# Causal attention and a cosine layer on one core: v loaded a step sooner, the last pair's transposes moved up

## Chip, core and metric

The kernel runs on one core of a Trainium2 chip. The metric is the device time of one execution in microseconds (us). TensorE (PE) multiplies and transposes; a transpose is a matmul with an identity matrix. VectorE (DVE), ScalarE (ACT) and GpSimd (POOL) work beside it, and SyncE (SP) only issues transfers between HBM and the on-chip memory. Each engine runs its own instructions in the order in which they are written; semaphores hold an engine back where it needs what another makes.

## What is computed

Two parts stand one behind the other: causal attention over 4 batches of 12 heads (448 tokens, 64 columns each), and a layer of two matrix products with g = h cos(h) between them.

```python
def _attn_ref(q, k, v):                         # (4, 12, 448, 64), float32
    scores = scale * np.matmul(q, k.transpose(0, 1, 3, 2))
    scores = np.where(mask, -1000000000.0, scores)
    scores = scores - np.max(scores, axis=-1, keepdims=True)
    attn = np.exp(scores)
    attn = attn / (np.sum(attn, axis=-1, keepdims=True) + 1e-09)
    return np.matmul(attn, v).astype(np.float32)

def _moe_ref(x, w_in, w_out):                   # x: (1792, 768), w_in: (768, 2048)
    h = x @ w_in
    g = h * np.cos(h)
    return (g @ w_out).astype(np.float32)
```

## The kernel before

The program is written out by hand: the order in the source is the order on each engine. `attention` is a generator; each `yield` ends a step, and the loop that drives it puts a piece of weight conversion for the second part behind each step.

The 4 x 12 heads make N = 24 pairs of heads. Step i works on three pairs at once:

- `scores(i)` (matmuls at L360), `masked` (DVE, L369: mask, running minimum) and `exps` (ACT, L376) make the probabilities of pair i in one of three tiles `pb`.
- `av(i - 2)` (L410) multiplies the transposed probabilities of pair i - 2 with its v, `divide` (DVE, L437 to L439) divides by the sums, `turn_out` (L448) transposes the outputs, and `finish` (ACT, L464 and L465) and `finish_hi` (POOL, L470 and L471) store them as x of the second part. The products, the ones column that gives the sums and the turned outputs all lie in PSUM banks 0 and 1.
- `transpose_in(i + 2)` (L316) transposes q and k of pair i + 2, which `evac_in` copies to SBUF in the next step.
- `tp(i - 1)` (L393) transposes the probabilities of pair i - 1 in two groups into PSUM, and `evac_tp` (L320 on DVE, L322 on ACT) copies them to a tile `pm`.

On TensorE a step is scores, av, transpose_in, tp, turn_out. Steps 0 to 2 are put together differently, since the pipeline fills. Behind the last scores, in steps 23 to 25, `fill` puts matmuls of the second part (the first 36, L570 to L572) between what is left of attention; step 26 runs the rest of these.

SP issues the loads. In step i stand `load_qk(i + 3)` (L257: two issues for k, two for q, 64 runs of partitions with pieces of 256 bytes, into one of three buffers in the tile `land`), `load_v(i - 1)` (L266: two issues into `vn`, one of three buffers; for even pairs also L273: two issues into `vo`, one of two buffers, for pairs i and i + 1), and behind them, from the driving loop, now and then a piece of a weight (L117, L122), a store of converted weights (L204, L206) or of raw ones (L1347). At the end of step 22 the driving loop adds two weight loads of 768 KB (L117) into `land`, and behind steps 23 to 25 ACT makes masks from them (L166, L168, L170).

Before step 0 `keep_warm` issues matmuls on a tile of zeros (L287).

Of the kernel before, what the change touches and what calls it, by code (L numbers as in the profile page):

```python
# [21 lines left out]
def kernel(  # L22
# [205 lines left out]
    def attention(filler_of, postponed):  # L228
        with (
# [19 lines left out]
            def half(h):  # L249
                return slice(h * R, (h + 1) * R)  # L250
# [34 lines left out]
            def keep_warm(n):  # L285
                for _ in range(n):
                    nc.tensor.matmul(  # L287
                        banks8[:, 0, 0:P], lhsT=warm, rhs=warm, start=True, stop=True
                    )

            keep_warm(44)
            ident = cst.tile([P, P], F32, name="ident")
            make_identity(nc, ident)

# [16 lines left out]
            def transpose_in(i, bs, order=None):  # L311
                for h in range(2):
                    qkt[i, h] = flat[:, 2 * h + i % 2, 0:S], banks8[:, bs[h], 0:S]
                for c, h in order or [(c, h) for c in range(NM) for h in range(2)]:
                    o = qkt[i, h][1].rearrange("p (r c) -> p c r", c=NM)
                    nc.tensor.transpose(o[:, c], nat[i][half(h), c], ident[half(h), half(h)])  # L316
# [7 lines left out]
            def evac_in(i, h, dve=False):  # L324
                evac(*qkt[i, h], dve)
# [14 lines left out]
            def open_step(i):  # L340
                prob[i] = prob_t[i % 3]
                stats[i] = at.tile([P, 8], F32, tag="stat", bufs=3, name="stat")
# [31 lines left out]
            def exps(i, *ms):  # L374
                for m in ms:
                    nc.scalar.activation(  # L376
                        probs(i, m), probs(i, m), AF.Exp, scale=-1.0, bias=stats[i][:, col(m)]
                    )
# [19 lines left out]
            def evac_tp(i, g, bs, h, dve=False):  # L398
# [2 lines left out]
                    banks8[:, bs[h], 0 : NM * R], dve,  # L401
                )

            def av(i):
                (vn, vo), pt = vals.pop(i), ptr[i]

                def add(m, j, y, lhsT, rhs, start=False, stop=False):
                    b, n, h = PLACE[m]
                    c = (2 * n + j) * E1
                    nc.tensor.matmul(  # L410
                        banks8[half(h), b, c : c + E1], lhsT=lhsT, rhs=rhs, start=start, stop=stop
                    )

                for j in range(2):
                    for y in range(2):
                        for a, ms in enumerate(LAST):
                            m, ys = ms[y], half(y)
                            g, n = spots[ms[0], NM]
                            add(
                                m, j, y, pt[ys, g, j ^ SWAP[m], n],  # L420
                                vo[ys, a, i % 2, j] if y else vn[ys, m // 2, j], start=j == 0,
                            )
                pieces = [(7, 6, k) for k in range(3)] + [(5, 4, k) for k in range(2)] + [(2, 3, 0)]
                for x, (ma, mb, k) in enumerate(pieces):
                    for j in range(2):
                        for m in (ma, mb):
                            g, n = spots[m, k]
                            add(
                                m, j, 0, pt[:, g, j ^ SWAP[m], n], vn[:, k, j],
                                stop=j == 1 and x in (2, 5),  # L430
                            )

            def divide(i):
                o = banks8[:, 0:2, 0 : 4 * E1].rearrange("p b (n e) -> p b n e", e=E1)
                r = at.tile([P, 2, 4, 1], F32, tag="r", bufs=2, name="r")
                t = outs[i] = at.tile([P, 2, 4, D], F32, tag="on", bufs=2, name="on")
                nc.vector.tensor_scalar(r, o[:, :, :, D:E1], 1e-9, None, op0=ALU.add)  # L437
                nc.vector.reciprocal(r, r)
                nc.vector.tensor_tensor(t, o[:, :, :, 0:D], r.to_broadcast([P, 2, 4, D]), op=ALU.mult)  # L439

            def turn_out(i):
                t = outs[i].rearrange("p b n d -> p b (n d)")
                for x in range(4):
                    for h, ms in enumerate((ROW[1::2], ROW[::2])):
                        if x < len(ms):
                            b, n, _ = PLACE[ms[x]]
                            c = (T0, 4 * R)[h] + x * R
                            nc.tensor.transpose(  # L448
                                banks8[:, 1 - h, c : c + R],
                                t[half(h), b, n * P : (n + 1) * P], ident[half(h), half(h)],  # L450
                            )

# [8 lines left out]
            def finish(i):  # L461
                xf = at.tile([P, S], F32, tag="xf", bufs=2, name="xf")
                x = xf.rearrange("p (n r) -> p n r", r=R)
                nc.scalar.copy(x[:, 1::2], banks8[:, 1, T0 : T0 + 3 * R].rearrange("p (n r) -> p n r", r=R))  # L464
                nc.scalar.copy(x[:, 0::2], banks8[:, 0, 4 * R : 8 * R].rearrange("p (n r) -> p n r", r=R))  # L465
                return xf

            def finish_hi(i, xf):
# [11 lines left out]
                    pass  # L480

            TB_ = (2, 3)
            transpose_in(0, TB_)
            evac_in(0, 1)
            evac_in(0, 0, True)
            keep_warm(10)
            load_v(0)
            for i in range(N + 4):
                cur, prev, old = i < N, 0 < i <= N, 0 <= i - 2 < N
                G1, G2 = (7, 4), (5, 6)  # L490
                if i == 1:
                    G1, G2 = (0, 1), TB_
                elif i >= N - 1:
                    G1, G2 = TB_, (4, 5)
                while postponed:
                    postponed.pop(0)()
                if i + 3 < N:
                    load_qk(i + 3)
                if 1 < i <= N:
                    load_v(i - 1)  # L500
                if cur:
                    open_step(i)
                    scores(i)
                if i == 0:
                    masked(i, 4, 3)
                    exps(i, 4, 3)
                    masked(i, 7, 6)
                    exps(i, 7)
                    transpose_in(1, TB_)
                    evac_in(1, 0, True)  # L510
                    evac_in(1, 1)
                    keep_warm(8)
                    exps(i, 6)
                    masked(i, 5, 1, 2)
                    exps(i, 5, 1, 2)
                    yield i
                    continue
                if i == 1:
                    transpose_in(2, TB_)
                    masked(i, 4, 3, 7, 6, 5, 1, 2)  # L520
                    exps(i, 4, 3)
                    evac_in(2, 0)
                    evac_in(2, 1)
                    exps(i, 7)
                elif cur:
                    if 2 < i < N - 1:
                        evac_in(i + 1, 0)
                        evac_in(i + 1, 1)
                    masked(i, 4, 3, 7, 6, 5, 1, 2)
                    exps(i, 4, 3, 7, 6, 5, 1, 2)  # L530
                    if i == 2:
                        transpose_in(3, TB_)
                        evac_in(3, 0, True)
                        evac_in(3, 1, True)
                if i == N + 2:
                    run(extra[0])
                if old:
                    av(i - 2)
                    divide(i - 2)
                if 1 < i < N - 2:  # L540
                    transpose_in(i + 2, TB_)
                if i == N:
                    fill(8)
                if prev:
                    open_ptr(i - 1)
                    tp(i - 1, 0, G1)
                    evac_tp(i - 1, 0, G1, 0, True)
                    evac_tp(i - 1, 0, G1, 1)
                    if i == 1:
                        exps(i, 6, 5)  # L550
                    tp(i - 1, 1, G2)
                    evac_tp(i - 1, 1, G2, 1)
                    evac_tp(i - 1, 1, G2, 0, i % 2 == 0 or i < 4)
                if i == 1:
                    exps(i, 1, 2)
                if N - 2 < i < N + 2:
                    fill((4, 4, 6)[i + 1 - N])
                if old:
                    turn_out(i - 2)
                    xf = finish(i - 2)  # L560
                    finish_hi(i - 2, xf)
                yield i

    def m1_sum(ring, g, fi, t0, n, hv):
        x, t = x_part(t0, n)
# [844 lines left out]
```

## Time and profile before

| | us |
|---|---|
| median of the three timed runs | 610.51 |
| the three runs | 607.86, 610.51, 611.37 |
| the profiled execution | 608.23 |
| its span, first to last instruction | 606.1 |

The profiled execution is some 2 us longer than its span: the span runs from the first to the last instruction. All times of rows are counted from the start of the span. Attention takes the first 165 us or so; the rest is the second part. The granted TensorE clock has a mean of 0.997 of full speed over the span.

### The profile page before, as it was taken

How to read it: one execution, taken by the hardware profiler on the slowest of the kernel's cores; microseconds unless marked ns; L12 is line 12 of the kernel's file. 1: busy time of each engine (PE TensorE's matmuls, PEld its weight loads, DVE VectorE, ACT ScalarE, POOL GpSimd, SP SyncE). 2: the span in 40 equal slices, each digit the busy share in tenths (PEclk: the TensorE clock that was granted, in tenths of full speed). 3: DMA queues.
4: the chain of work that ended last, by engine and by line, in shares of the span. 5: the costliest groups of instructions: out<-in, count | busy, mean ns of one | idle time of the engine just before them, and what ended most of it. 6: DMA issues, size and time to landing. Idle time of an engine off the chain costs nothing.

```text
span 606.1 us, 15320 instructions
## 1 busy us (share of the span) xinstructions
PE 587.0 (97%) x5912; PEld 544.5 (90%) x5912; DVE 454.7 (75%) x955; ACT 401.3 (66%) x785; POOL 398.3 (66%) x426
## 2 busy tenths in 40 slices
PE   8999898898999999999999999999999999999996
PEld 7888787787799989899999999999999999999996
DVE  5988698886477787877777777853387887887786
ACT  5999798987566797877778777732534644654540
POOL 0235344535258787877878777844579779878994
PEclk9999999999999999999999999999999999999999
DMA  8768667676037879796968878589988548648105
GB/s 158 161 156 183 162 154 201 156 181 175 10 131 247 300 211 339 241 351 194 345 239 284 297 228 322 193 303 391 391 331 292 195 149 303 209 158 305 58 1 156
DMA packets 127096, 134.30 MB, mean 222 GB/s; under 512 B 75152, under 2 KB 111360, under 8 KB 127024
## 3 DMA queue, kind: packets, MB, share of 16 engines
q1 hardware_dynamic: 118400, 106.69, 57.3%
q0 software_dynamic: 4928, 24.78, 11.1%
q10 hardware_dynamic: 3696, 1.87, 1.2%
q8 instruction: 46, 0.75, 0.5%
q14 instruction: 26, 0.21, 0.1%
HBM read 83.36 MB, written 49.94 MB: 220 GB/s over the span
## 4 chain that ended last, share of the span: by engine, by line
PE 73%; DVE 11%; DMA 8%; ACT 3%; SPq 3%; issue 2%; POOL 1%; DVEq 0%; ACTq 0%
PE banks L666 18%; PE banks L1115 12%; PE banks L1095 12%; PE banks L571 6%; PE banks L572 6%; PE banks L570 6%; PE banks L410 4%; PE banks L360 3%; DMA vo<-in_v_dram 2%; DVE pb L369 2%; PE banks L1132 2%; PE banks L1019 2%; DMA vn<-in_v_dram 2%; SPq L257 2%; DVE pm L320 2%
## 5 line engine op out<-in xcount | busy, mean ns | idle before, releaser
L654 DVE TENSOR_TENSOR acc<-acc,banks 128x768 f32<-128x768 f32 (+1 forms) x122 | 112.6, 932 | 43.1 <-PE banks L666 32.9
L666 PE MATMUL banks<-w,gh 128*128 128x384 f32 x512 | 110.0, 335 | 0.1
L666 PEld LDWEIGHTS banks<-w,gh 128*128 128x128 f32 x512 | 90.7, 188 | 2.2 <-DVE acc L654 0.8
L571 PE MATMUL banks<-xa,w 128*128 128x512 f32 x192 | 75.5, 393 | 0.0
L572 PE MATMUL banks<-xa,w 128*128 128x512 f32 x192 | 75.0, 391 | 0.0
L570 PE MATMUL banks<-xa,w 128*128 128x512 f32 x192 | 74.9, 390 | 0.0
L376 ACT ACTIVATE pb<-pb,stat 128x256 f32<-128x256 f32 (+6 forms) x168 | 71.4, 522 | 3.0 <-DVE stat L369 2.9
L666 PE MATMUL banks<-w,gl 128*128 128x384 f32 x256 | 65.1, 335 | 0.0
L369 DVE CUSTOM_DVE_ANT_0 pb<-banks,mask 128x256 f32<-128x256 f32 (+6 forms) x168 | 59.8, 420 | 5.0 <-PE banks L360 5.0
L690 POOL TENSOR_TENSOR w<-ct,w 128x768 fp32r<-128x768 f32 x28 | 51.9, 1853 | 16.0 <-ACT w L689 15.9
L470 POOL CAST xa<-xf 128x448 fp32r<-128x448 f32 (+1 forms) x18 | 9.6, 532 | 75.6 <-ACT xf L465 75.6
L578 ACT ACTIVATE ni<-banks 128x512 int32<-128x512 f32 (+1 forms) x64 | 34.4, 537 | 33.4 <-PE banks L572 20.2
L410 PE MATMUL banks<-vn,pm 128*64 128x65 f32 (+1 forms) x1344 | 51.3, 227 | 3.9 <-DMA vn<-in_v_dram 2.4
L597 POOL TENSOR_TENSOR gl<-r,gh 128x512 fp32r<-128x512 f32 x32 | 41.5, 1299 | 16.7 <-ACT gh L596 16.5
L580 DVE SCALAR_TENSOR_TENSOR r<-ni,banks 128x512 f32<-128x512 int32 (+1 forms) x56 | 35.0, 626 | 22.6 <-ACT ni L578 21.9
L410 PEld LDWEIGHTS banks<-vn,pm 128*64 128x64 f32 (+1 forms) x1344 | 46.2, 140 | 6.4 <-ACT pb L376 1.9
L582 ACT ACTIVATE r<-r 128x512 f32<-128x512 f32 (+1 forms) x56 | 32.8, 585 | 22.6 <-DVE r L580 22.0
L666 PEld LDWEIGHTS banks<-w,gl 128*128 128x128 f32 x256 | 46.4, 188 | 0.0
L585 DVE SCALAR_TENSOR_TENSOR r<-r,banks 128x512 f32<-128x512 f32 (+1 forms) x56 | 35.1, 626 | 13.6 <-ACT r L583 13.6
L1095 PE MATMUL banks<-xb,bb 128*128 128x384 f32 x234 | 44.8, 334 | 0.0
L360 PE MATMUL banks<-flat 64*64 64x64 f32 (+5 forms) x768 | 42.1, 356 | 2.1 <-ACT flat L322 0.6
L360 PEld LDWEIGHTS banks<-flat 64*64 64x64 f32 x768 | 32.7, 133 | 11.4 <-DVE pm L320 3.7
(142 smaller groups left out, 1445.2 us busy)
## 6 DMA issues: line engine op xcount, KB each, us to landing
bb<-w_in_d SPq DMA_DIRECT2D x48, 384.0 KB, 5.2
land<-in_moe_w_in_dram SPq DMA_DIRECT2D x14, 768.0 KB, 6.3
land<-in_moe_w_out_dram SPq DMA_DIRECT2D x14, 768.0 KB, 5.7
w_out_d<-w POOLq DMA_DIRECT2D x14, 768.0 KB, 5.8
big<-w_out_d SPq DMA_DIRECT2D x25, 384.0 KB, 5.2
w_in_d<-w POOLq DMA_DIRECT2D x7, 768.0 KB, 4.2
raw_d<-ct POOLq DMA_DIRECT2D x14, 384.0 KB, 7.5
land<-in_k_dram SPq DMA_DIRECT2D x45, 112.0 KB, 3.6
```

The lines of the kernel that those rows point to most:

```text
L360: nc.tensor.matmul(place(m)[heads(j ^ SWAP[m]), c : c + z - a], lhsT=qt[heads(j), (m - 1) * R : m * R], rhs=kt[heads(j), a:z], start=banks ...
L369: nc.vector.tensor_tensor_reduce(out=probs(i, m), in0=place(m), in1=mask[:, z : z + m * R], scale=-scale, scalar=3.0e38, op0=ALU.add, op1= ...
L376: nc.scalar.activation(probs(i, m), probs(i, m), AF.Exp, scale=-1.0, bias=stats[i][:, col(m)])
L410: nc.tensor.matmul(banks8[half(h), b, c : c + E1], lhsT=lhsT, rhs=rhs, start=start, stop=stop)
L570: yield nc.tensor.matmul(hv, lhsT=wh[:, f], rhs=x[:, 0, cc, t], start=(cc == 0), stop=False)
L571: yield nc.tensor.matmul(hv, lhsT=wh[:, f], rhs=x[:, 1, cc, t], start=False, stop=False)
L572: yield nc.tensor.matmul(hv, lhsT=wl[:, f], rhs=x[:, 0, cc, t], start=False, stop=(cc == NCC - 1))
L654: nc.vector.tensor_tensor(d, d, o, op=ALU.subtract)
L666: nc.tensor.matmul(o[:, e, 0:EH], lhsT=a[:, cs], rhs=w[:, e * EH : (e + 1) * EH], start=(x == 0), stop=(x == 5),)
L690: nc.gpsimd.tensor_tensor(w[:, 1], tf, f32(w[:, 0]), op=ALU.subtract)
L1095: nc.tensor.matmul(o, lhsT=w[:, u, k * P : (k + 1) * P], rhs=x[k][:, v], start=k + m == 0, stop=k == K - 1 and m == 2,)
L1115: nc.tensor.matmul(o[:, b % 2, 0:EH], lhsT=g_ops[i][u][:, c * P : (c + 1) * P], rhs=wouts[g, i][:, v], start=(x == 0), stop=(x == 2),)
```

## The change

There are three parts.

- `load_v(i)` is called in step i, where `load_v(i - 1)` was. The vn buffer of pair i was last read by av(i - 3), in step i - 1, so that the issue now has a wait on TensorE.
- Step 23 transposes the probabilities of pair 23 itself, behind the outputs of pair 21 and two fillers, group 1 into banks 4 and 5, group 0 into 2 and 3. The product of pair 23 and its turned output lie in banks 4 and 5 instead of 0 and 1 (`obank`). Then av(22), av(23), the outputs of pair 22, four fillers, the outputs of pair 23; the fillers that are left follow.
- In steps 0 to 2 some work changes places: k is transposed ahead of q, with zero matmuls behind each (32, 9, 8 and 6 where there were 44, 10 and 8), and the transposes of pair 0's probabilities stand in steps 1 and 2, a group in each.

```diff
-            keep_warm(44)
+            keep_warm(32)
...
+            def obank(i):
+                return 4 if i == N - 1 else 0
+
             def av(i):
-                (vn, vo), pt = vals.pop(i), ptr[i]
+                (vn, vo), pt, ob = vals.pop(i), ptr[i], obank(i)
...
+            def evac_out(i, g, bs, *dve):
+                for h in range(2):
+                    evac_tp(i, g, bs, h, h in dve)
+
+            def put_out(i):
+                turn_out(i)
+                finish_hi(i, finish(i))
...
                 if i + 3 < N:
                     load_qk(i + 3)
-                if 1 < i <= N:
-                    load_v(i - 1)
-                if cur:
-                    open_step(i)
-                    scores(i)
+                if i:
+                    load_v(i)
+                open_step(i)
+                scores(i)
...
+                if i == N - 1:
+                    fill(4)
+                put_out(i - 2)
+                if i == N - 1:
+                    fill(2)
+                    open_ptr(i)
+                    tp(i, 1, (4, 5))
+                    evac_out(i, 1, (4, 5), 0)
+                    tp(i, 0, TB_)
+                    evac_out(i, 0, TB_, 0)
                 yield i
+            take_postponed()
+            av(N - 2)
+            divide(N - 2)
+            yield N
+            take_postponed()
+            av(N - 1)
+            divide(N - 1)
+            put_out(N - 2)
+            fill(4)
+            put_out(N - 1)
+            yield N + 1
+            take_postponed()
+            run(extra[0])
```

On SP's queue, before, steps 18 to 20 read as follows: k and q of pair 21, vn of pair 17, a raw store and a weight piece, k and q of pair 22, vn and vo of pair 18, k and q of pair 23, vn of pair 19 (a number behind vn or vo names the buffer, x2 the two heads).

```order
L257 DMA land<-in_k_dram 64x7x64 x2
L257 DMA land<-in_q_dram 64x7x64 x2
L266 DMA vn_90<-in_v_dram 128x3x64 x2
L1347 DMA raw_d<-ct 128x256
L122 DMA st<-in_moe_w_out_dram 128x512
L257 DMA land<-in_k_dram 64x7x64 x2
L257 DMA land<-in_q_dram 64x7x64 x2
L266 DMA vn_88<-in_v_dram 128x3x64 x2
L273 DMA vo_92<-in_v_dram 64x4x64 x2
L257 DMA land<-in_k_dram 64x7x64 x2
L257 DMA land<-in_q_dram 64x7x64 x2
L266 DMA vn_89<-in_v_dram 128x3x64 x2
```

The same steps on SP's queue in the changed kernel, from k and q of pair 21 to vn and vo of pair 20.

```order
L257 DMA land<-in_k_dram 64x7x64 x2
L257 DMA land<-in_q_dram 64x7x64 x2
L266 DMA vn_88<-in_v_dram 128x3x64 x2
L273 DMA vo_92<-in_v_dram 64x4x64 x2
L1379 DMA raw_d<-ct 128x256
L122 DMA st<-in_moe_w_out_dram 128x512
L257 DMA land<-in_k_dram 64x7x64 x2
L257 DMA land<-in_q_dram 64x7x64 x2
L266 DMA vn_89<-in_v_dram 128x3x64 x2
L257 DMA land<-in_k_dram 64x7x64 x2
L257 DMA land<-in_q_dram 64x7x64 x2
L266 DMA vn_90<-in_v_dram 128x3x64 x2
```

The vn and vo of pair 18 (vn_88, vo_92) stood behind q of pair 22 and now stand ahead of its k.

On TensorE, before, in step 24: the last fillers ahead of the transposes of pair 23's probabilities (pb_160), these, four fillers, the turned outputs of pair 22 and the start of the product of pair 23 (vn_90).

```order
L572 MATMUL banks<-xa,w_500 128x512
L570 MATMUL banks<-xa,w_500 128x512
L571 MATMUL banks<-xa,w_500 128x512
L572 MATMUL banks<-xa,w_500 128x512
L393 MATMUL banks<-ident,pb_160 128x64 x28
L570 MATMUL banks<-xa,w_500 128x512
L571 MATMUL banks<-xa,w_500 128x512
L572 MATMUL banks<-xa,w_500 128x512
L570 MATMUL banks<-xa,w_500 128x512
L448 MATMUL banks<-ident,on 128x64 x7
L410 MATMUL banks<-vn_90,pm 64x65 x2
L410 MATMUL banks<-vo_92,pm 64x65 x2
```

In the changed kernel, from the last of four fillers and the turned outputs of pair 21 in step 23 to the start of the product of pair 23 (L602 to L604 are the fillers, L452 the turned outputs, L413 the product; the tile pb_148 is that of pair 23).

```order
L602 MATMUL banks<-xa,w_497 128x512
L452 MATMUL banks<-ident,on 128x64 x7
L603 MATMUL banks<-xa,w_497 128x512
L604 MATMUL banks<-xa,w_497 128x512
L393 MATMUL banks<-ident,pb_148 128x64 x28
L413 MATMUL banks<-vn_89,pm 64x65 x2
L413 MATMUL banks<-vo_92,pm 64x65 x2
L413 MATMUL banks<-vn_89,pm 64x65 x2
L413 MATMUL banks<-vo_92,pm 64x65 x2
L413 MATMUL banks<-vn_89,pm 64x65 x24
L413 MATMUL banks<-vn_90,pm 64x65 x2
L413 MATMUL banks<-vo_92,pm 64x65 x2
```

The transposes of pair 23 moved ahead of the product of pair 22, and the two last products stand one behind the other.

## Rows read from the trace of the kernel before

**Rows 1.** Page, section 1: engine, busy us, share of span, instructions.

```profile
PE 587.0 (97%) x5912; PEld 544.5 (90%) x5912; DVE 454.7 (75%) x955; ACT 401.3 (66%) x785; POOL 398.3 (66%) x426
```

**Rows 2.** Busy by stretch, TensorE: stretch, length, busy (count), granted clock, DMA share, GB/s.

```profile
160.00:300.00 140.00, 139.87 (x708) 1.00 0.74 247
```

**Rows 3.** TensorE in order of time: start, us, line, out<-in, count [idle before <-releaser].

```profile
21.96 1.75 PE L360 MATMUL banks<-flat 64*64 64x256 f32 x32
...
92.47 1.75 PE L360 MATMUL banks<-flat 64*64 64x256 f32 x32
...
95.94 0.65 PE L316 MATMUL banks<-ident,land 64*128 64x64 f32 x14
...
97.84 1.75 PE L360 MATMUL banks<-flat 64*64 64x256 f32 x32
...
101.46 0.27 PE L410 MATMUL banks<-vo,pm 64*64 64x65 f32 x1 [1.47 <-DMA vo<-in_v_dram]
...
127.59 0.65 PE L316 MATMUL banks<-ident,land 64*128 64x64 f32 x14
...
129.49 1.75 PE L360 MATMUL banks<-flat 64*64 64x256 f32 x32
```

**Rows 4.** SP's issues in order of time, steps 15 and 19.

```profile
92.11 1.29 SPq L257 DMA_DIRECT2D land<-in_k_dram  x2
93.45 1.28 SPq L257 DMA_DIRECT2D land<-in_q_dram  x2
94.78 2.02 SPq L266 DMA_DIRECT2D vn<-in_v_dram  x2
96.84 1.27 SPq L273 DMA_DIRECT2D vo<-in_v_dram  x2
...
118.15 1.29 SPq L257 DMA_DIRECT2D land<-in_q_dram  x2
```

**Rows 5.** One line, L257, 21 to 126 us: count, ns min/median/max, first and last.

```profile
L257 SPq EVENT_SEMAPHORE  x18: 17/17/17, 21.4 to 122.4; - x18
```

**Rows 6.** Transfers issued from 118.1 to 119.4: count, KB, median us to landing.

```profile
land<-in_q_dram SPq DMA_DIRECT2D x2, 112.0 KB, 4.3
```

**Rows 7.** TensorE in order of time, the tail.

```profile
143.80 1.09 PE L393 MATMUL banks<-ident,pb 64*128 64x64 f32 x28
...
147.16 0.33 PE L410 MATMUL banks<-vn,pm 64*64 64x65 f32 x4 [0.75 <-ACT xf L465]
148.13 0.59 PE L410 MATMUL banks<-vo,pm 64*64 64x65 f32 x3 [0.64 <-DMA vo<-in_v_dram]
...
157.36 0.27 PE L410 MATMUL banks<-vn,pm 64*64 64x65 f32 x2 [0.75 <-ACT xf L465]
...
159.30 0.50 PE L571 MATMUL banks<-xa,w 128*128 128x512 f32 x1
...
160.89 0.46 PE L448 MATMUL banks<-ident,on 64*128 64x64 f32 x7
161.28 0.50 PE L571 MATMUL banks<-xa,w 128*128 128x512 f32 x1
...
164.59 0.39 PE L570 MATMUL banks<-xa,w 128*128 128x512 f32 x1
```

**Rows 8.** Busy by stretch, TensorE, the tail (columns as in rows 2).

```profile
145.00:148.80 3.80, 2.38 (x27) 1.00 0.74 115
148.80:152.30 3.50, 3.50 (x56) 0.51 0.02 5
```

**Rows 9.** ACT in order of time, step 23.

```profile
144.76 1.37 ACT L322 COPY pm<-banks 128x448 f32<-128x448 f32 x3
...
146.72 0.38 ACT L465 COPY xf<-banks 128x256 f32<-128x256 f32 x1
```

**Rows 10.** SP's weight loads, and landing of transfers issued from 138.5 to 143.4.

```profile
137.56 0.97 SPq L117 DMA_DIRECT2D land<-in_moe_w_in_dram  x2
...
vn<-in_v_dram SPq DMA_DIRECT2D x4, 96.0 KB, 7.0
```

More of the change, by code (lines that the diff above doesn't have):

```diff
@@ L410, in add @@
                     nc.tensor.matmul(
-                        banks8[half(h), b, c : c + E1], lhsT=lhsT, rhs=rhs, start=start, stop=stop
+                        banks8[half(h), ob + b, c : c + E1], lhsT=lhsT, rhs=rhs, start=start, stop=stop
                     )
@@ L433, in divide @@
             def divide(i):
-                o = banks8[:, 0:2, 0 : 4 * E1].rearrange("p b (n e) -> p b n e", e=E1)
+                ob = obank(i)
+                o = banks8[:, ob : ob + 2, 0 : 4 * E1].rearrange("p b (n e) -> p b n e", e=E1)
                 r = at.tile([P, 2, 4, 1], F32, tag="r", bufs=2, name="r")
@@ L448, in turn_out @@
                             nc.tensor.transpose(
-                                banks8[:, 1 - h, c : c + R],
+                                banks8[:, obank(i) + 1 - h, c : c + R],
                                 t[half(h), b, n * P : (n + 1) * P], ident[half(h), half(h)],
@@ L463, in finish @@
                 x = xf.rearrange("p (n r) -> p n r", r=R)
-                nc.scalar.copy(x[:, 1::2], banks8[:, 1, T0 : T0 + 3 * R].rearrange("p (n r) -> p n r", r=R))
-                nc.scalar.copy(x[:, 0::2], banks8[:, 0, 4 * R : 8 * R].rearrange("p (n r) -> p n r", r=R))
+                ob = obank(i)
+                for e, (b, c) in ((1, (1, T0)), (0, (0, 4 * R))):
+                    o = banks8[:, ob + b, c : c + (4 - e) * R]
+                    nc.scalar.copy(x[:, e::2], o.rearrange("p (n r) -> p n r", r=R))
                 return xf
@@ L482, in attention, with take_postponed @@
             TB_ = (2, 3)
[L483 to L494, printed above, removed]
+            def evac_out(i, g, bs, *dve):
[4 more added lines that the diff above has]
+                finish_hi(i, finish(i))
+            def take_postponed():
                 while postponed:
                     postponed.pop(0)()
+            transpose_in(0, TB_, [(c, 1) for c in range(NM)])
+            evac_in(0, 1)
+            keep_warm(9)
+            transpose_in(0, TB_, [(c, 0) for c in range(NM)])
+            evac_in(0, 0, True)
+            keep_warm(8)
+            load_v(0)
+            for i in range(N):
+                take_postponed()
                 if i + 3 < N:
                     load_qk(i + 3)
-                if 1 < i <= N:
-                    load_v(i - 1)
-                if cur:
-                    open_step(i)
-                    scores(i)
+                if i:
+                    load_v(i)
+                open_step(i)
+                scores(i)
                 if i == 0:
-                    masked(i, 4, 3)
+                    masked(i, 4, 3, 7)
                     exps(i, 4, 3)
-                    masked(i, 7, 6)
-                    exps(i, 7)
                     transpose_in(1, TB_)
@@ L511, in attention @@
                     evac_in(1, 1)
[L512 to L515, printed above, removed]
+                    keep_warm(6)
+                    masked(i, 6, 5, 1, 2)
+                    exps(i, 7, 6, 5, 1, 2)
                     yield i
@@ L523, in attention @@
                     evac_in(2, 1)
+                    open_ptr(0)
+                    tp(0, 0, (0, 1))
                     exps(i, 7)
-                elif cur:
-                    if 2 < i < N - 1:
+                    evac_out(0, 0, (0, 1), 0)
+                    exps(i, 6, 5, 1, 2)
+                    yield i
+                    continue
+                if i == 2:
+                    tp(0, 1, (0, 1))
+                    masked(i, 4, 3)
+                    evac_out(0, 1, (0, 1), 0)
+                    exps(i, 4, 3)
+                    transpose_in(3, TB_)
+                    masked(i, 7, 6, 5, 1, 2)
+                    exps(i, 7, 6, 5, 1, 2)
+                    evac_in(3, 0, True)
+                    evac_in(3, 1, True)
+                else:
+                    if i < N - 1:
                         evac_in(i + 1, 0)
@@ L530, in attention @@
                     exps(i, 4, 3, 7, 6, 5, 1, 2)
[L531 to L540, printed above, removed]
-                    transpose_in(i + 2, TB_)
-                if i == N:
-                    fill(8)
@@ L544, in attention @@
[L544 to L561, printed above, removed]
-                yield i
+                av(i - 2)
+                divide(i - 2)
+                if i < N - 2:
+                    transpose_in(i + 2, TB_)
+                G1, G2 = ((7, 4), (5, 6)) if i < N - 1 else (TB_, (4, 5))
+                open_ptr(i - 1)
+                tp(i - 1, 0, G1)
+                evac_out(i - 1, 0, G1, 0)
+                tp(i - 1, 1, G2)
@@ new lines, in attention @@
+                evac_tp(i - 1, 1, G2, 1)
+                evac_tp(i - 1, 1, G2, 0, i % 2 == 0)
+                if i == N - 1:
[8 more added lines that the diff above has]
+                    evac_out(i, 0, TB_, 0)
+                yield i
+            take_postponed()
@@ L564, in m1_sum @@
+            av(N - 2)
[8 more added lines that the diff above has]
+            yield N + 1
+            take_postponed()
+            run(extra[0])
+            yield N + 2
+            take_postponed()
+            yield N + 3
     def m1_sum(ring, g, fi, t0, n, hv):
```

## The prediction

> **What bounds the kernel now.** I first read busy times by engine: TensorE (PE) is busy 97% of the span [rows 1], and the table by stretches says where it is not. From 160 us on, in the second half of the program, it works 139.87 of 140 us at the full clock [rows 2]. So whatever makes the attention part and its hand-over end sooner should come off the end of the program one for one, as long as the other engines keep up there. What can be won lies before 165 us.
>
> Then the steps. One step without a wait goes from the scores of 92.47 to those of 97.84, 5.37 us; its transposes of q and k (L316) come 3.47 us after its scores [rows 3]. From step 3 (21.96) to step 21 (129.49) there are 18 steps in 107.53 us, where 18 x 5.37 = 96.7 would do: 10.8 us are lost, and the row at 101.46 names the usual reason, 1.47 us for the tile vo, which comes from v. The obvious reading is that v is asked for too late.
>
> The third view is SP's own queue. It shows why v is late: SP issues all of these loads, and does nothing else. In step 15 the pairs of issues for k, q, vn and vo stand with 0.04 to 0.06 us between them (92.11 + 1.29 ends at 93.40, the next starts at 93.45) [rows 4]. The row for the waits that stand ahead of the k loads says that none of the 18 in steps 3 to 20 lasted more than 17 ns [rows 5]: SP never waits for TensorE, it is just late. An issue takes some 0.62 us (half of 1.28), a step has four of q and k, two of vn, every other step two of vo, and a weight piece or a store now and then. So I read SP's issuing as the pace of steps 3 to 20, and TensorE's waits as its echo.
>
> **v one step sooner.** Nothing is removed from SP's list: the same loads stand there in another order. That alone removes the waits on v, because a pair's v is now issued one step earlier, 107.53 / 18 = 6.0 us, where the wait shown is 1.47 us. But each q and k now stands behind the v of one more pair: for an even pair behind two vn and two vo (1.27 us for the two vo in the row at 96.84, taken for vn too, and 0.04 between issues: 2.6 us), for an odd one behind 1.3 us. What is late next is therefore q and k. The last even pair decides, since after it TensorE's 5.37 us per step is the slower: its q (pair 22) was issued from 118.15, the second at 118.8, and landed 4.3 us later by the median of the two [rows 4, 6], at 123.1. Behind 2.6 us more it lands at 125.7. Its transposes started at 127.59 [rows 3]. So TensorE can come 1.9 us sooner in step 20, and no more; of the 10.8 us lost some 9 stay, now ahead of L316. Bounds: every wait gone would be 10.8; a DMA that lands 1 us later than before leaves 0.9. The new wait of a v load for the product that last read its buffer (pair i-3, in the step before) stands ahead of the next q and k on SP. SP reaches it about 2.7 us into its step i; that product is over 3.5 us into step i-1, so it has some 4.6 us to spare, and as TensorE comes no further ahead than its q and k let it, I cost it at nothing. If the cover went, each microsecond there would delay q and k by as much.
>
> The Trainium skill's page "DMA: Bandwidth & Descriptors" gives another price: under "Rules for kernel authors" it advises to issue a DMA early and wait for it late, so that its fixed cost is hidden, and under "Issuing engines are not separate DMA queues" it calls the sequencer's time for starting a DMA usually small beside the DMA. By that the move hides all waits and rival B below holds; by the rows here 0.62 us of issuing, eight times a step, is not small beside 5.37.
>
> **First three steps and warm-up.** At 5.37 us a step, TensorE starting step 3 at 21.96 would reach the transposes of pair 22 at 21.96 + 17 x 5.37 + 3.47 = 116.7, nine microseconds before 125.7. So these steps can become some microseconds shorter or up to nine longer with no effect on the end. SP's list up to there does not depend on them. Zero; bounds -0.5 and +0.5.
>
> **The tail.** From the transposes of pair 22's probabilities (143.80) to the first matmul behind the 36 fillers (164.59) before takes 20.79 us [rows 7]. Within it TensorE waits 0.75 us at 147.16, 0.64 at 148.13 and 0.75 at 157.36, and then the clock falls: from 148.8 to 152.3 the granted clock is 0.51 after a stretch in which TensorE worked 2.38 of 3.80 us [rows 8], which is the lower level of 1.2 GHz and costs half of 3.5 us, 1.7. The work itself is unchanged: two groups of transposes of 1.05 us, 36 fillers of 0.236 (14 from 161.28 to 164.59), three turns of outputs of 0.39 (160.89 to 161.28), two products of 1.94 (157.36 to 159.30) and 0.4 for going from one kind to the other: 2.1 + 8.5 + 1.2 + 3.9 + 0.4 = 16.1 [rows 7]. Gain 4.7 if no wait is left.
>
> Is one left? On the clock of before: the first turn of outputs ends near 146.3, two fillers at 146.9. The last pair's transposes into banks 4 and 5 need ScalarE's (ACT's) last copy out of them; its three copies from 144.76 end at 146.13 [rows 9]: 0.8 us to spare. They run to 147.9; the product of pair 22 needs banks 0 and 1, which ACT leaves at 147.10: 0.8 to spare, and that is the wait of 0.75 us gone. The next product writes banks 4 and 5 and needs no such thing: the other 0.75. v of pair 23 is still issued behind the two weight loads of 768 KB at 137.56; what was issued there landed 7.0 us later [rows 10]. With TensorE and SP some 2 us sooner it lands near 144 and is wanted near 147.8. The copies of the last pair stand ahead of the masks on ACT. Nothing in the sum is later; I take 4.7, and 2.0 as the low bound (clock falls again, one wait stays).
>
> **Sum.** 1.9 + 4.7 = 6.6 us. The profiled execution took 608.23 with a span of 606.1; 608.23 - 6.6 = 601.6. The median of the three timed runs is 610.51, 2.3 higher, and gives 603.9. I put the forecast between, at 602.5.
>
> **Rivals.** A is the forecast. B: SP is not the limit, and all of the 10.8 us go: 608.2 - 10.8 - 4.7 = 592.7. It is also what the skill's rule above would make of the change. For it: the waits carry v's name. Against it: rows 4 and 5. C: the tail gives little, because v of pair 23 lands after 147.8 behind the weight loads and the clock falls as before; 0.2 to 2 us come from there, and with the 1.9 it is about 606. For it: 7.0 us of landing there; against it: some 3.8 us to spare. D: nothing reaches the end, because VectorE, ACT or GpSimd set the pace of the second half: 608.2. Against it: TensorE without a gap for 140 us [rows 2]. E, slower: the waits for q and k fall on the even pairs, some 1.2 us each (SP needs 2 x 5.97 us for two steps, TensorE 2 x 5.37), and each makes the clock fall as at 148.8. A fall costs 1.7 us there, so four falls eat the 6.6 and eight, one per even pair from 8 to 22, give 608.2 - 6.6 + 13.6 = 615. Against it: the wait of 1.47 us at 101.46 left the clock at full; for it: 1.4 us of idle time in two pieces at 147 to 148 did not.
>
> **Chances.** A 0.60, B 0.12, C 0.13, D 0.08, E 0.07. The time is A's. B and E together are 0.19, so the range reaches from A's lower end (602.5 less the 5 us by which SP or the tail may do better) to D: 597.5 to 608.5. 0.5%, about 3 us, is what a measurement of this kernel can tell from no change. Faster by more: A and B, 0.72; within: C and D, 0.21; slower: E, 0.07.
>
> **What would show it.** Right: no waits left for vo and vn, but waits of L316 for q of some 8 to 9 us in all; SP's issues still back to back until about 127; transposes of pair 22 near 125.7; no stretch of half clock near 149; the first matmul behind the 36 fillers 6 to 7 us sooner, near 158; TensorE without a gap after it. Wrong: step 21's scores before 124, which is B; a wait for v of pair 23, which is C; a granted clock near 0.5 in steps 5 to 20, which is E; gaps of TensorE between 165 and 300, which is D.

## The result, and the profile after

| | median, us | runs | against before, beside it | 95% interval |
|---|---|---|---|---|
| before | 610.42 | 4 | | |
| changed | 602.29 | 4 | 0.9875 | 0.984 to 0.9909 |
| before, later | 607.16 | 23 | | |
| changed, later | 603.98 | 12 | 0.9942 | 0.9916 to 0.9968 |

The change is faster. The first comparison says by 7.6 us (0.0125 x 610.4), the later and longer one, made with the experiments below, by 3.5 us (1.9 to 5.1). The two intervals do not meet. The later one has more runs, and the first took the kernel before at 610.42 where its medians on the three later occasions (7 to 35 runs each) are 606.2 to 607.4; I lean on the later one. The profiled execution of the changed kernel took 603.45 us with a span of 601.6, against 608.23 and 606.1 before: 4.8 us less. I account for those 4.8.

First the list of what TensorE waited for, by line; columns are the sum in us, how often, and the longest. Before:

```profile
PE banks L410 <- DMA vo<-in_v_dram: 4.3, 6, 1.5
PE banks L410 <- DMA vn<-in_v_dram: 2.4, 4, 0.9
...
PE banks L316 <- DMA land<-in_q_dram: 0.6, 1, 0.6
```

After, the same list has neither v tile; its first line is

```profile
PE banks L316 <- DMA land<-in_q_dram: 7.9, 4, 2.7
```

The waits for v (6.7 us) are gone, and waits for q of about their size stand in their place. TensorE in order of time after (start, length, line, count, idle time and what ended it), the rows that answer [rows 3] and [rows 7]:

```profile
22.64 0.67 PE L360 MATMUL banks<-flat 64*64 64x256 f32 x10
...
127.29 0.74 PE L316 MATMUL banks<-ident,land 64*128 64x64 f32 x14 [2.68 <-DMA land<-in_q_dram]
...
129.16 1.31 PE L360 MATMUL banks<-flat 64*64 64x256 f32 x20
...
143.46 1.09 PE L393 MATMUL banks<-ident,pb 64*128 64x64 f32 x28
...
147.83 0.27 PE L413 MATMUL banks<-vn,pm 64*64 64x65 f32 x2
...
151.72 0.46 PE L452 MATMUL banks<-ident,on 64*128 64x64 f32 x7
...
153.24 0.47 PE L452 MATMUL banks<-ident,on 64*128 64x64 f32 x7
...
159.66 0.39 PE L602 MATMUL banks<-xa,w 128*128 128x512 f32 x1
```

Step 3 starts 0.7 us later than in [rows 3], and the transposes of pair 22 0.3 us sooner (127.29 for 127.59); so 0.3 us is all that the steps gave. The tail, from 143.46 to 159.66, takes 16.20 us where [rows 7] has 20.79, with no wait in it: 4.6 us. The busy table by stretches shows the rest (stretch, length, busy time and count of TensorE, its weight loads, VectorE, ACT and GpSimd, then granted clock, DMA share, GB/s):

```profile
98.00:101.50 3.50, 1.77 (x64) 1.56 (x54) 2.87 (x15) 3.09 (x8) 2.68 (x5) 1.00 0.67 156
101.50:105.00 3.50, 3.37 (x59) 3.28 (x63) 1.61 (x4) 1.52 (x5) 0.00 (x0) 0.59 0.89 230
144.00:160.00 16.00, 16.00 (x233) 12.97 (x230) 9.16 (x19) 12.27 (x23) 8.15 (x11) 1.00 0.21 62
160.00:300.00 140.00, 139.15 (x701) 125.86 (x700) 106.04 (x132) 105.33 (x159) 105.78 (x98) 1.00 0.77 259
```

The stretch of half clock at 148.8 in [rows 8] is gone, 1.00 throughout the tail. One fall came at 101.5 instead, behind a stretch with 1.77 us of work in 3.5, as rival E has it, but once and not eight times. From 160 to 300 us TensorE works 139.15 us, 0.7 less than in [rows 2], and the second half gives 0.4 us back up to the end of the span. Sum: 0.3 + 4.6 - 0.4, and 0.3 outside the span, are the 4.8.

SP's rows after (a line's operations with count, ns min/median/max, first and last start), and its issues for q of pair 22:

```profile
L266 SPq DMA_DIRECT2D vn<-in_v_dram x36: 384/560/1808, 19.6 to 123.9; - x36
L266 SPq EVENT_SEMAPHORE  x34: 17/17/17, 27.0 to 123.9; - x34
```

```profile
L257 SPq EVENT_SEMAPHORE  x18: 17/17/17, 23.9 to 124.4; - x18
```

```profile
121.85 1.29 SPq L257 DMA_DIRECT2D land<-in_q_dram  x2
```

The new waits of the v loads are there, 34 of them. That none lasted over 17 ns says nothing, neither here nor in [rows 5]: such a row does not hold the time that SP waits. In merge_q, an experiment below, SP does wait for the product that last read a vn buffer: its issues of 50.86 begin 3.8 us behind the end of the issue before them (46.17 + 0.89). The row of these waits has 17 ns throughout all the same:

```profile
46.17 0.89 SPq L257 DMA_DIRECT2D land<-in_q_dram  x1
50.86 1.26 SPq L272 DMA_DIRECT2D vn<-in_v_dram  x2
```

```profile
L272 SPq EVENT_SEMAPHORE  x36: 17/17/17, 24.1 to 117.6; - x36
```

That SP hardly ever waits is shown by the pauses between its records: from 22 to 122 us none is longer than 0.46 us after, and 0.44 before. And the product that last read a vn buffer had ended 5.0 us or more ahead of the issue into it (pairs 3 to 21). Nor do the new waits cost SP anything else that shows: the issue behind one is as much shorter (560 ns for the 614 of the row before) as the pause ahead of it is longer (98 ns for 44, all medians).

```profile
L266 SPq DMA_DIRECT2D vn<-in_v_dram x37: 480/614/1880, 19.0 to 126.0; - x37
```

But q of pair 22 is issued 3.7 us later than in [rows 4], where the prediction had 2.6. The second load of it stands in the chain of work that ended last, with its start and the time until it landed:

```profile
122.52 4.63 DMA land<-in_q_dram
```

### The profile page after: what moved, and what is told of

Same layout as the page of the kernel before. It is cut to its first block, busy times and chain, and to the rows that moved or that the text cites. A ratio compares the mean times of both kernels' runs of the same rounds, so it can differ in the third digit from the quotient of the medians.

```text
span 601.6 us, 15347 instructions
## 1 busy us (share of the span) xinstructions
PE 583.0 (97%) x5905; PEld 542.1 (90%) x5905; DVE 455.9 (76%) x954; ACT 402.4 (67%) x786; POOL 398.4 (66%) x426
## 4 chain that ended last, share of the span: by engine, by line
PE 76%; DVE 11%; DMA 6%; ACT 3%; issue 2%; SPq 1%; POOL 1%; DVEq 0%; ACTq 0%; POOLq 0%
PE banks L698 18%; PE banks L1147 12%; PE banks L1127 12%; PE banks L603 6%; PE banks L602 6%; PE banks L604 6%; DVE pb L369 4%; PE banks L360 4%; PE banks L413 3%; DMA land<-in_q_dram 3%; PE banks L1164 2%; PE banks L1051 2%; PE banks L393 2%; PE banks L316 2%; DVE pm L320 2%
## 5 line engine op out<-in xcount | busy, mean ns | idle before, releaser
L604 PE MATMUL banks<-xa,w 128*128 128x512 f32 x192 | 75.0, 391 | 0.0
L602 PE MATMUL banks<-xa,w 128*128 128x512 f32 x192 | 74.9, 390 | 0.0
L413 PE MATMUL banks<-vn,pm 128*64 128x65 f32 (+1 forms) x1344 | 47.6, 223 | 0.5 <-DVE pm L320 0.5
L413 PEld LDWEIGHTS banks<-vn,pm 128*64 128x64 f32 (+1 forms) x1344 | 44.2, 137 | 2.4 <-issue 0.6
```

The lines of the kernel that those rows point to most:

```text
L413: nc.tensor.matmul(banks8[half(h), ob + b, c : c + E1], lhsT=lhsT, rhs=rhs, start=start, stop=stop)
L602: yield nc.tensor.matmul(hv, lhsT=wh[:, f], rhs=x[:, 0, cc, t], start=(cc == 0), stop=False)
L604: yield nc.tensor.matmul(hv, lhsT=wl[:, f], rhs=x[:, 0, cc, t], start=False, stop=(cc == NCC - 1))
```

## The experiments

Each kernel ran beside the kernel before on the same occasion (607.43, 606.19 and 607.16 us), and ratios are against that. "Pair 22" is the start of the transposes of its probabilities (143.80 before), "tail" the time from there to the first matmul behind the fillers (20.79 before), both read in the trace of one profiled execution of each.

| kernel | median, us | ratio, 95% interval | pair 22 | tail |
|---|---|---|---|---|
| v_alone | 607.92 | 1.0004, 0.998 to 1.0028 | 145.13 | 18.09 |
| v_back | 603.43 | 0.9929, 0.9904 to 0.9954 | 143.10 | 16.06 |
| first_back | 605.44 | 0.9972, 0.9947 to 0.9998 | 143.90 | 16.08 |
| first_back2 | 605.20 | 0.9955, 0.9925 to 0.9986 | 147.38 | 16.35 |
| bank0 | 607.27 | 1.0009, 0.9978 to 1.0039 | 145.78 | 18.79 |
| after_2 (changed) | 603.98 | 0.9942, 0.9916 to 0.9968 | 145.91 | 16.08 |
| merge_q | 594.78 | 0.9805, 0.9757 to 0.9853 | 138.76 | 16.36 |
| merge_q2 | 595.00 | 0.9814, 0.9773 to 0.9855 | 136.40 | 16.07 |
| mq_first | 594.95 | 0.9805, 0.977 to 0.984 | 135.29 | 16.17 |
| mq_before | 598.09 | 0.9862, 0.9804 to 0.992 | 134.76 | 18.61 |
| pool_v | 596.24 | 0.981, 0.9757 to 0.9864 | 136.16 | 17.13 |
| split_k | 616.51 | 1.016, 1.0109 to 1.0212 | 156.29 | 16.07 |

### The parts of the change, one at a time

v_alone is the kernel before with

```diff
-                if 1 < i <= N:
-                    load_v(i - 1)
+                if 0 < i < N:
+                    load_v(i)
```

> The kernel before with only the loads of v one step sooner. By the prediction's term as it was written: 1.9 us off, about 608.5 beside 610.4. By what the trace of after suggests instead (the transposes of pair 22 started only 0.3 us sooner, because SP's issuing sets the pace and each of v's loads now has a wait ahead of it on SP): no more than 0.5 us off, about 610. By rival B (SP is not the limit) 10 us off, about 600. Each of the first two says that the waits for vo and vn are gone from the list of waits and that waits of L316 for q of some 8 us stand there instead. The tail stays as before, with its stretch of half clock near 149.

v_back is the changed kernel with that undone, and `load_v(N - 1)` again ahead of the product of pair 22.

> The changed kernel with the loads of v put back to where they were; what is left is the reordered first three steps and the tail. The theory says that the tail is worth 4.6 us by itself, and the first steps nothing: 605 to 606 beside 610.4 and 602.3, with TensorE's waits for vo and vn back and none for q. Rival: the tail needs v of the last pair sooner, and without it waits for it; then 1 to 3 us of the tail's gain go and it is near 607 to 608. If the gain of the two parts is not a sum (v alone 0.3, tail alone 4.6, together 8.1 by the medians), something that both touch is still to be found.

first_back is the changed kernel with the first three steps and the warm-up of before, run on two occasions.

> The changed kernel with the first three steps and the warm-up in the order of before; v sooner and the tail stay. The theory says that these steps end long before SP's issuing lets TensorE go on, so that nothing reaches the end: 602.3 with at most 0.5 either way, the scores of step 3 up to 1 us sooner or later and the transposes of pair 22 at the same place. Rival: the order of the first steps sets when the buffers of q and k come free for SP's next loads, and moves the whole chain of loads: then the time differs by 1 us or more and so does the start of the q loads of pair 22.

> The changed kernel once more, for a comparison with the same runs of the kernel before as the kernels beside it. The parts, as run apart, came to 0 us for v alone, 4.3 us for first steps and tail together, and 1.7 us for v and tail together; the whole came to 7.6 us in its first four runs. If the parts are right, the whole is worth 4 to 5 us: 602.5 to 603.5 where the kernel before takes 607.4. If the first runs are right, it is 600 there, and the three parts help one another in a way that none of the runs apart shows.

> The changed kernel with the first three steps of before, once more and beside the changed kernel itself. If the first steps are worth nothing, the two come out within 1 us of each other. If the 605.4 of its first runs stands beside some 602.5 to 603.5 for the changed kernel, the first steps are worth 2 to 3 us, which the prediction put at 0 with a bound of 0.5.

v sooner by itself is worth nothing: 1.0004, with at most 1.2 us by the interval. Rival B falls with it. Its list of waits has the waits for q in place of those for v, and v_back's has those for v in place of those for q, at a time no worse than the changed kernel's (0.9929 beside 0.9942). v_alone's line, then v_back's:

```profile
PE banks L316 <- DMA land<-in_q_dram: 10.3, 7, 2.5
```

```profile
PE banks L413 <- DMA vo<-in_v_dram: 3.3, 4, 1.4
PE banks L413 <- DMA vn<-in_v_dram: 1.4, 1, 1.4
...
PE banks L316 <- DMA land<-in_q_dram: 0.7, 1, 0.7
```

In six profiled executions with v sooner and the same number of issues, the changed kernel's two among them, pair 22 starts between 143.46 and 147.38; in the two with v where it was, at 143.10 and 143.80. If the move does anything to the steps, it is not a gain.

It also goes with more stretches of half clock. In five of these six executions the granted clock falls to about half for some 3.5 us or more between 65 and 135 us (at 101.5 after, 128 in after_2, 126.5 in first_back, 67 and 104.5 in bank0, 103.5 and 127 in first_back2); v_back has two such stretches as well (65 and 102.5), v_alone and the kernel before none. And of the 64 runs with v sooner and as many issues, 4 have a mean granted clock of 0.999 or more over the span, of the 65 later runs of the kernel before 20, of v_back's 12 there are 3. What those stretches cost at the end is not shown.

v_back holds the first steps and the tail, and comes to 4.3 us, all of the gain that the longer comparison finds. The parts then do add up: 0 and 4.3 beside 3.5 (1.9 to 5.1). first_back, which holds v and the tail, comes to 1.7 us (0.1 to 3.2) on one occasion and 2.7 (0.9 to 4.5) on the other. On the first it stands 2.0 us behind v_back; on the second, at 605.2, 1.2 us behind the changed kernel's 603.98, with intervals that overlap. That the first steps are worth nothing is neither refuted nor shown to better than some 2 us, and no kernel here holds the tail alone.

v_alone has another thing to tell, since its tail has the instructions of before. TensorE in its tail, and the busy table there:

```profile
145.13 1.09 PE L393 MATMUL banks<-ident,pb 64*128 64x64 f32 x28
...
148.49 0.28 PE L410 MATMUL banks<-vn,pm 64*64 64x65 f32 x2 [0.75 <-ACT xf L465]
...
155.98 0.27 PE L410 MATMUL banks<-vn,pm 64*64 64x65 f32 x2 [0.75 <-ACT xf L465]
...
163.22 0.39 PE L570 MATMUL banks<-xa,w 128*128 128x512 f32 x1
```

```profile
146.40:150.10 3.70, 2.95 (x63) 2.29 (x64) 1.33 (x4) 3.32 (x7) 1.52 (x2) 1.00 0.43 112
150.10:153.60 3.50, 3.50 (x56) 2.78 (x50) 1.36 (x4) 0.38 (x2) 1.27 (x3) 1.00 0.00 0
```

The two waits of 0.75 us stand there as in [rows 7], but the wait for vo of 0.64 does not, TensorE worked 2.95 us of 3.7 where [rows 8] has 2.38 of 3.8, and the clock stayed at 1.00: 18.09 us in place of 20.79. mq_before, whose tail is also that of before, has 18.61. So the tail of before takes 20.8 us in the execution in which the clock falls, and 18.1 to 18.6 in these two, in which neither the fall nor the wait for vo is there; the new tail is worth 4.6 us beside the one and 2.0 to 2.5 beside the others. The 3.5 and 4.3 us measured lie between.

That the kernel before itself also runs without the fall is shown by the mean granted clock of its runs. A stretch of 3.5 us at 0.51 takes the mean over 606 us down to 0.997, by estimate, and that is what the profiled execution has; 20 of the 65 later runs have 0.999 or 1.000, so no such stretch anywhere. In how many of the other 45 one falls in the tail is not shown.

### The last pair's banks

bank0 is the changed kernel with

```diff
-                return 4 if i == N - 1 else 0
+                return 0
```

> The changed kernel with the product of the last pair in banks 0 and 1, as all other pairs have it, in place of 4 and 5. The theory says that the product of the last pair then waits for the division of pair 22's product, as it did before (0.75 us), and no clock falls: 0.7 to 1.3 us more than the changed kernel, 603 to 603.6. Rival: the wait brings the stretch of half clock back, 1.7 us more on top, 604.7 to 605.3. A second rival: the fillers cover it, no change.

Nothing of the gain is left by its ratio, 1.0009, and at most 1.3 us by the interval: 4.1 us more than the changed kernel, where 0.7 to 1.3 were expected. TensorE in its tail:

```profile
145.78 1.09 PE L393 MATMUL banks<-ident,pb 64*128 64x64 f32 x28
...
153.36 0.27 PE L413 MATMUL banks<-vn,pm 64*64 64x65 f32 x2 [1.35 <-DVE on L443]
...
156.61 0.46 PE L452 MATMUL banks<-ident,on 64*128 64x64 f32 x7 [1.23 <-DVE on L443]
...
164.57 0.39 PE L602 MATMUL banks<-xa,w 128*128 128x512 f32 x1
```

The tail is 18.79, 2.6 more than after, in two waits. The first is the expected one, 1.35 us in place of 0.75. The second, 1.23, was not expected: the turned outputs of pair 22 go into the banks that the product of pair 23 then still holds, and wait for its division. The clock stays full in the tail. Moving the transposes without the banks is thus worth no more than the tail of before with full clock (18.09). The 4.1 us between this kernel and the changed one (1.0009 for 0.9942) come from two occasions and are known to some 2.4 us either way, an estimate from the two intervals, so the 2.6 us of the tail may be all of it; the steps of this execution are no later than those of others with the same loads (145.78 beside 143.46 and 145.91).

### Is SP's issuing the pace?

merge_q loads both heads of a pair's q with one DMA, and of k (6 issues in place of 8 in a step that loads vo, 4 in place of 6 in the others):

```diff
-                    for j, eng in enumerate(engs or (nc.sync, nc.sync)):
+                    if not engs:
+                        nc.sync.dma_start(
+                            out=nat[i][half(h)].rearrange("p c (j d) -> p c j d", j=2),
+                            in_=src[b, 2 * hp : 2 * hp + 2].rearrange("j (p c) d -> p c j d", c=NM),
+                        )
+                        continue
+                    for j, eng in enumerate(engs):
```

> The changed kernel with the loads of the two heads of a pair's q in one DMA in place of two, and of its k too (from pair 3 on): 6 issues a step on SP in place of 8, the same bytes. If the price of SP's issuing is one for each DMA (0.62 us), 1.2 us a step come free, SP is faster than TensorE's 5.37 us per step, the waits of L316 for q vanish, and the attention part ends some 7 to 9 us sooner: 593 to 595. If the price goes with the descriptors of a DMA, the merged issue takes 1.2 us and nothing changes: 602. A third way: the transfer is slower when it writes both heads' columns in turn, lands later, and the waits grow: over 603.

mq_before has the same edit in the kernel before, pool_v issues vn from GpSimd, split_k cuts one load of q in two.

> The kernel before, v not sooner and the tail as it was, with the two heads' loads of q (and of k) in one DMA. If the waits for vo and vn were an echo of SP's issuing, they vanish although v is issued in the same step as before, and it takes some 9 to 10 us less than before: 600 to 602. If v was simply asked for too late, the waits for vo and vn stay: 609 to 610.

> The changed kernel with the two loads of vn of each pair from pair 2 on issued by GpSimd in place of SP: the same 8 DMAs a step, 6 of them on SP. If SP's issuing is the pace, the waits for q vanish as with the merged loads: 593 to 597. If it is the transfers themselves, shared by both queues, that are late, nothing changes: 602. A rival on the other side: GpSimd has its own work in these steps and issues v late, so that waits for vn come back: 603 to 608.

> The changed kernel with one of the four loads of q and k of each pair from pair 3 on cut into two DMAs of half the size: one more issue a step on SP, the same bytes and descriptors. If a DMA's issue has a price of its own (0.62 us) and SP sets the pace of some 18 steps, it costs 18 x 0.6 = 11 us: 613. If the price goes with the descriptors, 0 to 2 us: 602 to 604.

> The changed kernel with the two heads' loads of q, and of k, in one DMA, once more beside the changed kernel. By its first runs 8 us less than the changed kernel, 594.8.

> The merged loads of q and k with the first three steps of before in the changed kernel; v sooner and the tail stay. With SP no longer the pace, TensorE's own steps count from the first one on, so that the order of the first three steps is no longer free: the scores of step 3 came at 21.9 with the steps of before and merged loads, at 23.4 with those of after. If that reaches the end, it is 1 to 1.5 us less than the merged loads alone, some 593.5. If the first steps of after had done work ahead that those of before leave for later, it is the same within 0.5 us, or up to 1 us more.

Taking issues off SP gives what moving v did not: merge_q 0.9805 and 0.9814 where the changed kernel has 0.9942, about 8 us more, and pool_v the same in another way by its ratio (0.981; 6.5 us by its median). One issue a step more costs 18 x 0.6 = 11 us by the expectation; against the changed kernel (0.9942 x 606.2 = 602.7) it is 13.8, known to some 3.5 either way. (split_k's two pieces cover six of the seven chunks of that load, so a seventh of one head's q is not loaded.) SP's issues in merge_q, both heads at a time:

```profile
L257 SPq DMA_DIRECT2D land<-in_k_dram x18: 595/601/1695, 22.7 to 114.9; - x18
L257 SPq DMA_DIRECT2D land<-in_q_dram x18: 682/694/2628, 23.3 to 115.6; - x18
```

and in split_k, the two pieces of one head's q (L259), then the whole load of the other head:

```profile
L259 SPq DMA_DIRECT2D land<-in_q_dram x37: 606/617/1444, 20.6 to 140.0; - x37
```

```profile
L264 SPq DMA_DIRECT2D land<-in_q_dram x18: 592/608/1537, 21.9 to 135.9; - x18
```

Three chunks of a head's seven take 617 ns, one head 608, two heads 601 (k) and 694 (q): on SP the price goes by the DMA, and hardly by its size. The Trainium skill's page "DMA: Bandwidth & Descriptors" says, under "Issuing engines are not separate DMA queues", that starting DMAs from more engines saves only the sequencer's time for it, usually small beside the DMA. Here that saving was all there was to have: pool_v moves the same bytes, by that page through the same 16 engines, and is 6 to 8 us faster than the changed kernel.

mq_before answers what the waits for v were. There v is loaded when it always was, and 0.3 us is left of the 6.7:

```profile
PE banks L322 <- DMA land<-in_q_dram: 0.7, 1, 0.7
PE banks L416 <- DMA vo<-in_v_dram: 0.3, 1, 0.3
```

The busy table for 22 to 127 us, after, then pool_v, then merge_q2:

```profile
22.00:127.00 105.00, 96.60 (x2580) 86.38 (x2575) 90.97 (x369) 96.14 (x243) 48.00 (x75) 0.98 0.70 164
```

```profile
22.00:127.00 105.00, 103.21 (x2803) 92.34 (x2803) 97.32 (x395) 101.88 (x259) 79.31 (x115) 1.00 0.82 184
```

```profile
22.00:127.00 105.00, 102.86 (x2798) 92.23 (x2800) 96.95 (x395) 101.23 (x258) 50.77 (x78) 1.00 0.87 182
```

TensorE's idle time there falls from 8.4 us to 1.8 and 2.1. pool_v pays a little of it back in the tail, 17.13, with one wait for v of the last pair (the rival for GpSimd being late, in small):

```profile
143.25 0.27 PE L413 MATMUL banks<-vn,pm 64*64 64x65 f32 x2 [0.86 <-DMA vn<-in_v_dram]
```

mq_first differs from mq_before by v and the tail alone: 0.9805 for 0.9862, 3.5 us, with intervals that overlap; the tails of the two traces are 2.4 us apart (16.17 and 18.61). From merge_q2 it differs by the first steps alone, and not in time (0.9805 for 0.9814): its step 3 starts at 21.39 for 23.99 and pair 22 1.1 us sooner, less than these intervals tell apart. The version that beats both kernels is merge_q, at 595.0 beside 603.98 on one occasion; with either order of the first steps it comes out the same.

## Why the prediction was right, and where it was not

**What bounds the kernel: right, and now shown.** Fewer issues on SP, with v not moved, take the waits for v away; one issue more makes all later. Of the two rows on which the prediction put this, the issues back to back [rows 4] bear it; the 17 ns of [rows 5] do not, since such a row stays at 17 ns where SP does wait. v's name on the waits was the echo that the prediction took it for.

**v, 1.9 us: wrong by its size.** It is 0.3 in the one pair of traces and 0 in v_alone. The exchange of waits came as told (7.9 us at L316, 8 to 9 forecast). The step that failed is "Behind 2.6 us more it lands at 125.7": q of pair 22 came 3.7 us later on SP, not 2.6, and took 4.6 to land (122.52 to 127.15), not 4.3; 1.4 us together, and pair 22 started at 127.29. That is not the scatter of one execution: its second load is issued at 118.81 and 118.87 in the two executions with v where it was, and at 122.5 to 125.4 in the six with v sooner, each time more than 2.6 later. The new waits, costed at nothing, show no cost, and the long issues of SP, below, differ from execution to execution; where those further 1.1 us and more lie stays open. The bound of 0.9 below was too tight.

**First steps, 0 with a bound of 0.5: not settled**, see first_back; by themselves they show 1.2 us, and 2.0 where v differs too (first_back beside v_back).

**Tail, 4.7: right in the traces (4.59), too large for runs in which the clock does not fall.** The price by kind came out at 16.20 for 16.1. What it is measured against is the point: the prediction took the clock fall of [rows 8] as part of every execution. It is part of some: 20 of 65 runs of that kernel are without it, and in two traces without it the gain is 2.0 to 2.5.

**Second half: right.** The 0.4 us given back is no sign of D: from the first matmul behind the fillers to the end of the span it is 441.6 us before and 442.0 after, but 441.3 in after_2, the changed kernel again, and 440.7 to 443.6 over all executions here.

**The sum**, 6.6, lies between the two comparisons, 7.6 and 3.5, and well above the second's upper end. So that the time, 602.5, agrees with the first median of 602.29 is luck: of its two terms one is nothing, and the other counts a fall of the clock that not every run has. Of the rivals, B is refuted by v_alone and C by the rows of the tail. E's falls came, once after (at 101.5) and once or twice in four of the five other executions with v sooner, but not eight times, and the kernel did not become slower. That the later wait for q, 2.68 us at 127.29, would have been longer without the fall at 101.5 is argued, not shown.

## What to carry to other kernels

The name on a wait tells which load was late, not why: look at the queue that issues it, and if that queue stands without gaps, a load moved forward only moves the wait to the next tile. To see whether the queue waits, look at the pauses between its records and not at how long a record of a wait is. Then count issues, not bytes: join loads or give some to another engine. And before a stretch of half clock is put into a sum, see in a second execution whether it is there.

## What the runs showed of the hardware

SP's issues are not alike. Between 22 and 127 us the changed kernel has 20 of over 0.95 us among 137, where the median is some 0.6; together they take 14.6 us more than 0.62 each, a seventh of the stretch. Each of the 20 lies over the fetch of a block on the queue for instructions (21 fetches in that time); in the kernel before it is 17 of 17, with 21 fetches. One pair of issues after, and the transfers by queue for 119.4 to 120.9 us (packets, MB, share):

```profile
119.57 2.22 SPq L257 DMA_DIRECT2D land<-in_k_dram  x2
```

```profile
q8 instruction: 1, 0.02, 5.6%
```

The page of the profile has for the whole program:

```profile
q8 instruction: 46, 0.75, 0.5%
```

The Trainium skill's page "Runtime: NRT & Kernel Launch", under "Instruction fetch mechanics", says that an engine's instructions come in blocks of 16 KiB, 256 at a time, at a cost that is mostly hidden. By that the 46 blocks are 11,776 instructions, and TensorE's matmuls and weight loads are 5905 and 5905, 11,810: an estimate from that page's figure says that these are TensorE's own blocks. If the fetch is what stretches SP's issues, which are on the path here, the page's "mostly hidden" leaves out this cost to another engine. That the fetch is the cause, and not a companion, was not tried.
